# w2's raw pieces in the pool of h's loads and taps, loaded two half steps sooner

## The chip, the cores and the metric

The kernel runs on one core of one Trainium2 chip. The metric is device microseconds of one launch on that core, the median of several runs.

## What is computed

The reference adds three things for one sequence of S = 2048 rows and D = 448 columns: its input `x`, a long-convolution branch, and a two-layer MLP. F is 1792.

```python
xn = _layernorm(x)
# A: short causal convolution of k (4 taps), times v, long causal convolution by FFT, gate
k_shift = sum(k_pad[:, t:t + S, :] * shift_k[:, ks - 1 - t] for t in range(ks))
kv = k_shift * v
y = irfft(rfft(kv) * rfft(ssm_k))[:S] + kv * ssm_D
a = xn * y
# B: dense, mish, dense
h = xn @ w1 + b1
b = (h * tanh(softplus(h))) @ w2
out = x + a + b
```

## The kernel before

**Steps.** The work is cut along the MLP. The sequence is 8 chunks of 256 rows, F is 7 pairs of two 128-wide blocks, and (chunk, pair) makes 56 steps. Each step has two half steps, numbered from 0: an even half step 2i runs `g1_mm` of step i (first dense layer, 22 matmuls), the odd one 2i+1 runs `mish` of step i and then `g2_mm` of step i-2 (second dense layer, 12 matmuls; `G2_LAG = 2`). All the rest, that is layer norm, the transforms of h (the kernel `ssm_k`, transposed) and of kv, the taps and the output gate, is hung on half steps by two tables: `at(s, ...)` puts a function ahead of the MLP's work of half step s, `after(s, ...)` puts it behind. The program is recorded in that order and each engine works through its own instructions in it; nothing reorders them later.

**Split weights.** TensorE multiplies in a rounded 32-bit type. Each weight is therefore split into a rounded part and a rest: ScalarE casts the raw piece (`w1_hi` L340, and the cast of `split` L74), VectorE subtracts (`w1_lo` L345 and L347, `split` L75). w1 and w2 come in 7 raw pieces each, one per pair; in this text w1[p] and w2[p] are the pieces of pair p. The split of w1[p] stands at half step 2p-2, ahead of `g1_mm` of step p. The split of w2[p] stands behind half step 2p+3, ahead of `g2_mm` of step p in half step 2p+5. All of this happens in chunk 0; later chunks find the weights in place.

**Pools.** Raw pieces of w1, w2 and later the pieces of k share `kr`, four buffers. Pool `x` has seven buffers for h's loads, v's loads, the taps' products and `sD`. A buffer is handed on in the order in which buffers are given back, and the load that takes it over waits for the last reader of the old content.

**Queues and their semaphores.** SyncE (SP) issues nearly all loads in program order; ScalarE (ACT) issues, in between its own arithmetic, the stores of the transformed h to the scratch array `Dh` (`f1_out` L140, two DMAs each, three half steps after the transform's matmuls). A DMA signals its end on one of eight semaphores, DMAHW0 to DMAHW7. The DMAs of SP and ACT take them in turn, in program order, whatever their queue, and a DMA waits for the one that had its semaphore before, unless that wait has been made already. So each DMA may have to wait for the landing of the eighth DMA ahead of it, and behind a DMA that waits stands everything that its engine has to issue after it.

**Half steps around the change.** `f1_mm` of h's pieces (L125) in chunk 0: h[1] at half step 1, h[2] at 4, h[3] at 8, h[0] at 12. ScalarE copies and VectorE adds and subtracts the result (`f1_fold`, L131, L132, L134), and `f1_out` stores it at 4, 7, 11 and 15.

The functions touched are `w2_load` and the loop over the pairs at the end of the function:

Of the kernel before, what the change touches and what calls it, by code (L numbers as in the profile page):

```python
# [14 lines left out]
S, D, F = 2048, 448, 1792  # L15
# [23 lines left out]
def tile_kernel(ctx: ExitStack, tc, q, k, v, sk, hT, sD, w1, b1, w2, c_f1, c_g, c_gi, c_i2, out):  # L39
# [51 lines left out]
    def at(slot, fn, *args):  # L91
        plan.setdefault(int(slot), []).append((fn, args))

    def after(slot, fn, *args):
        plan2.setdefault(int(slot), []).append((fn, args))
# [7 lines left out]
    def xt():  # L103
        return sp1.tile([128, 2, D], F32, name="x", bufs=7)

    def kr():
        return sp1.tile([128, 4, CH], F32, name="kr", bufs=4)
# [225 lines left out]
    RW = {}  # L333
# [17 lines left out]
        w1_lo(p)  # L351

    def w2_load(p):
        RW["2", p] = rw = kr().rearrange("p a b -> p (a b)")[:, :2 * D].rearrange("p (a b) -> p a b", a=2)
        nc.sync.dma_start(rw, w2[:, 2 * p:2 * p + 2])

    def w2_split(p):
# [198 lines left out]
    for p in range(NP):  # L556
        if p >= 2:
            at(max(2 * p - 5, 0), w1_load, p)
        if p >= 1:
            at(2 * p - 2, w1_split, p)  # L560
        p and at(2 * p + (1 if p < 5 else 0), w2_load, p)
        after(2 * (p + G2_LAG) - 1, w2_split, p)

    for o in range(NO):
# [46 lines left out]
    w1_load(1)  # L611
    nc.sync.dma_start(b1t, b1)
    w2_load(0)
    h_load(2)
    stats, aggr, eps, power, norm, tail = ln_parts(0)
# [99 lines left out]
```

## Time and profile before

| | |
|---|---|
| runs | median 369.93 us of 3 (369.01 to 371.45) |
| the profiled execution | 370.86 us, of which 368.9 us lie between its first and last instruction |
| TensorE matmul (PE) | 360.9 us busy, 98% |
| TensorE weight load (PEld) | 292.6 us, 79% |
| VectorE (DVE) | 262.5 us, 71% |
| ScalarE (ACT) | 166.3 us, 45% |
| GpSimd (POOL) | 71.2 us, 19% |
| DMA | 79.35 MB, mean 215 GB/s |

The page gives each engine's busy time in a profiled execution of 368.9 us. PE's matmuls are pipelined and their ends are modelled, so 98% busy means that nearly no gap between matmuls is left, and not that each runs at its best. Rows of the time line give start, duration, engine, line and operation, output and inputs, and in brackets the idle time ahead of the row with what ended it. The letter q behind an engine (ACTq, SPq) marks its queue of instructions: an issue of a DMA, or a wait. "DMA kr" in a row of the chain is a transfer into a `kr` buffer.

### The profile page before, as it was taken

What the parts mean: (1) busy time and instruction counts of PE and PEld (TensorE: products, weight loads), DVE (VectorE), ACT (ScalarE), POOL (GpSimd) and SP (SyncE); (2) the same over time, 40 slices, a digit from 0 to 9 for tenths busy, and PEclk for the clock granted to TensorE, in tenths of its full rate; (3) what the DMA queues carried; (4) which work ended last, traced back from release to release, by engine and by line L of the source; (5) the groups of instructions that cost most, each with busy time, mean ns of one, the idle gap of its engine ahead of it and who ended that gap; (6) DMA issues with size and microseconds to landing.
All of it is one profiled execution on the core that took longest, in us unless ns stands there. A gap on an engine that the chain in (4) does not pass through costs nothing.

```text
span 368.9 us, 7464 instructions
## 1 busy us (share of the span) xinstructions
PE 360.9 (98%) x3128; PEld 292.6 (79%) x3128; DVE 262.5 (71%) x359; ACT 166.3 (45%) x277; POOL 71.2 (19%) x58
## 2 busy tenths in 40 slices
PE   7998999999999999999999999999999999999995
PEld 2697888978888989889868666666666889889885
DVE  5897858999998888996515657656385752897751
ACT  3757543344241443253254555556655533235450
POOL 2005000920228222611006000060000005102020
PEclk9999999999999999999999999999999999999999
DMA  7998996839496329514675598896694375949655
GB/s 241 346 285 312 358 368 184 256 105 295 105 299 214 89 66 274 170 48 101 225 244 174 194 261 238 282 301 189 209 292 125 95 248 205 419 195 276 116 66 133
DMA packets 32354, 79.35 MB, mean 215 GB/s; under 512 B 2881, under 2 KB 19138, under 8 KB 32322
## 3 DMA queue, kind: packets, MB, share of 16 engines
q1 hardware_dynamic: 20210, 44.09, 35.8%
q10 hardware_dynamic: 9776, 22.88, 22.2%
q0 software_dynamic: 2336, 11.93, 11.3%
q8 instruction: 24, 0.39, 0.4%
q14 instruction: 8, 0.07, 0.1%
HBM read 50.44 MB, written 28.44 MB: 214 GB/s over the span
## 4 chain that ended last, share of the span: by engine, by line
PE 71%; DMA 12%; DVE 9%; POOL 3%; ACT 2%; issue 2%; SPq 0%; ACTq 0%; POOLq 0%; DVEq 0%
PE pg L457 27%; PE pg L482 10%; PE pg L484 9%; PE pg L483 9%; PE pc L208 7%; DMA kr<-in_w_dram 6%; PE pc L251 4%; PE pc L125 2%; PE pc L308 2%; DMA Dh<-st 2%; DVE x L172 2%; PE pg L407 2%; POOL xn L392 2%; DMA Dkv<-st 1%; DMA av<-Dkv 1%
## 5 line engine op out<-in xcount | busy, mean ns | idle before, releaser
L465 ACT ACTIVATE a<-pg,b1t 128x256 f32<-128x256 f32 x112 | 47.1, 472 | 113.0 <-PE pg L457 88.2
L457 PE MATMUL pg<-XH,w1h 128*128 128x256 f32 x448 | 91.3, 285 | 0.9 <-ACT XH L419 0.9
L75 DVE TENSOR_TENSOR acl<-a,ach 128x512 fp32r<-128x512 f32 x56 | 38.8, 693 | 65.0 <-ACT ach L74 64.7
L457 PEld LDWEIGHTS pg<-XH,w1h 128*128 128x128 f32 x448 | 69.6, 188 | 18.9 <-issue 15.7
L482 PE MATMUL pg<-w2h,ach 128*128 128x448 f32 x224 | 83.1, 371 | 0.0
L483 PE MATMUL pg<-w2l,ach 128*128 128x448 f32 x224 | 81.3, 363 | 0.9 <-DVE w2l L75 0.9
L484 PE MATMUL pg<-w2h,acl 128*128 128x448 f32 x224 | 81.4, 363 | 0.0
L457 PE MATMUL pg<-XL,w1h 128*128 128x256 f32 x448 | 69.6, 277 | 0.2 <-DVE XL L417 0.2
L457 PEld LDWEIGHTS pg<-XL,w1h 128*128 128x128 f32 x448 | 59.4, 188 | 0.4 <-DVE XL L417 0.4
L457 PE MATMUL pg<-XH,w1l 128*128 128x256 f32 x336 | 56.8, 277 | 0.0
L482 PEld LDWEIGHTS pg<-w2h,ach 128*128 128x128 f32 x224 | 42.0, 188 | 11.7 <-issue 9.4
L457 PEld LDWEIGHTS pg<-XH,w1l 128*128 128x128 f32 x336 | 46.8, 188 | 0.0
L483 PEld LDWEIGHTS pg<-w2l,ach 128*128 128x128 f32 x224 | 42.1, 188 | 3.6 <-DVE w2l L75 1.2
L484 PEld LDWEIGHTS pg<-w2h,acl 128*128 128x128 f32 x224 | 42.1, 188 | 2.5
L388 POOL TENSOR_TENSOR rstd<-ve,mhalf 128x2 f32<-128x2 f32 (+1 forms) x9 | 8.8, 977 | 156.2 <-DVE ve L385 156.1
L74 ACT CAST ach<-a 128x512 fp32r<-128x512 f32 x56 | 34.7, 620 | 1.8
L155 POOL TENSOR_TENSOR x<-kr,skb 128x896 f32<-128x896 f32 x8 | 17.1, 2133 | 83.6 <-DVE x L154 62.4
L392 POOL TENSOR_SCALAR xn<-qt,mv,rstd 128x448 f32<-128x448 f32 x12 | 27.8, 2320 | 0.6
L172 DVE TENSOR_TENSOR x<-x 128x896 f32<-128x896 f32 x24 | 26.8, 1115 | 1.4 <-POOL x L155 0.9
L131 ACT COPY st<-pc 128x896 f32<-128x896 f32 x16 | 14.5, 906 | 14.5 <-PE pc L125 12.6
L132 DVE TENSOR_TENSOR st<-pc,st 128x896 f32<-128x896 f32 x16 | 17.4, 1088 | 3.6 <-ACT st L131 3.1
L259 ACT COPY qe<-pc 128x896 f32<-128x896 f32 x16 | 13.8, 912 | 11.0 <-PE pc L251 10.8
(70 smaller groups left out, 389.7 us busy)
## 6 DMA issues: line engine op xcount, KB each, us to landing
Dh<-st ACTq DMA_DIRECT2D x16, 448.0 KB, 6.4
Dkv<-st ACTq DMA_DIRECT2D x16, 448.0 KB, 5.1
ah<-Dh SPq DMA_DIRECT2D x8, 896.0 KB, 7.0
av<-Dkv SPq DMA_DIRECT2D x8, 896.0 KB, 6.2
E<-qe ACTq DMA_DIRECT2D x16, 448.0 KB, 5.2
e<-E POOLq DMA_DIRECT2D x8, 896.0 KB, 7.9
kr<-in_k_dram SPq DMA_DIRECT2D x10, 448.0 KB, 6.7
x<-in_v_dram SPq DMA_DIRECT2D x8, 448.0 KB, 5.2
```

Of the source, the lines that this page charges most:

```text
L74: nc.scalar.copy(h, raw)
L75: V.tensor_sub(l, raw, h)
L132: V.tensor_add(st[:, 0], e, st[:, 1])
L155: nc.gpsimd.tensor_mul(o, KR[g - u // 2], skb[:, u:u + 1].to_broadcast([128, 2, D]))
L172: V.tensor_add(KV[g], KV[g], o)
L208: nc.tensor.matmul(p[32 * t:32 * t + 32, r, :D], g[rs, t, c], a[rs, t], start=True, stop=True, tile_position=(64 * r, 32 * t))
L392: eng.tensor_scalar(xn[:, jj, :D], Q[c][:, jj], mv[:, j, 0:1], rstd[:, j:j + 1], op0=ALU.subtract, op1=ALU.mult)
L457: nc.tensor.matmul(ps[:, n], l, r, start=n_ == 0, stop=n_ == len(mm) - 1)
L465: nc.scalar.activation(a[:, n], ps[:, n], AF.Mish, bias=b1t[:, 2 * p + n:2 * p + n + 1])
L482: nc.tensor.matmul(ps, ah[:, n, cs], w2h[:, f], start=f == 0, stop=False)
L483: nc.tensor.matmul(ps, ah[:, n, cs], w2l[:, f], start=False, stop=False)
L484: nc.tensor.matmul(ps, al[:, n, cs], w2h[:, f], start=False, stop=f == NF - 1)
```

## The change

w2's raw pieces are taken from pool `x` instead of `kr`, in the same shape, and the load of piece p (1 to 6) stands at half step 2p-1. Before, it stood at 2p+1 for p up to 4 and at 2p for 5 and 6. The load of piece 0, ahead of the loop, changes its pool alone. The splits stay where they are, and no arithmetic changes.

```diff
     def w2_load(p):
-        RW["2", p] = rw = kr().rearrange("p a b -> p (a b)")[:, :2 * D].rearrange("p (a b) -> p a b", a=2)
+        RW["2", p] = rw = xt()
         nc.sync.dma_start(rw, w2[:, 2 * p:2 * p + 2])
...
-        p and at(2 * p + (1 if p < 5 else 0), w2_load, p)
+        p and at(2 * p - 1, w2_load, p)
```

What it does to SP's row of loads, from w2[0] on: before (names ending in numbers are buffers; kr_119 is w2[0], x_121 is h[2], kr_163 is w1[2], qt_165 is the input rows of chunk 1, kr_200 is w1[3], x_239 is h[3], kr_241 is w2[1], kr_243 is w1[4], kr_296 is w2[2]; in brackets the semaphores that a row waits for, the number behind the underscore being the same for all):

```order
L355 DMA kr_119<-in_w2_dram 128x896 [waits DMAHW0_49]
L111 DMA x_121<-in_hT_dram 128x896 [waits DMAHW1_49]
L337 DMA kr_163<-in_w1_dram 128x1024 [waits DMAHW2_49]
L366 DMA qt_165<-in_q_dram 128x896 [waits DMAHW3_49]
L337 DMA kr_200<-in_w1_dram 128x1024 [waits DMAHW4_49,DVE_49,Activation_49]
L111 DMA x_239<-in_hT_dram 128x896 [waits DMAHW5_49]
L355 DMA kr_241<-in_w2_dram 128x896 [waits DMAHW6_49,DVE_49,Activation_49]
L337 DMA kr_243<-in_w1_dram 128x1024 [waits DMAHW2_49,DMAHW7_49,DVE_49,Activation_49]
L355 DMA kr_296<-in_w2_dram 128x896 [waits DMAHW1_49,DMAHW0_49,DVE_49]
```

And in the changed kernel (x_119 is w2[0], x_200 is w2[1], kr_202 is w1[3], x_241 is h[3], x_243 is w2[2], kr_245 is w1[4], x_298 is w2[3], kr_300 is w1[5]):

```order
L355 DMA x_119<-in_w2_dram 128x896 [waits DMAHW0_49]
L111 DMA x_121<-in_hT_dram 128x896 [waits DMAHW1_49]
L337 DMA kr_163<-in_w1_dram 128x1024 [waits DMAHW2_49]
L366 DMA qt_165<-in_q_dram 128x896 [waits DMAHW3_49]
L355 DMA x_200<-in_w2_dram 128x896 [waits DMAHW4_49]
L337 DMA kr_202<-in_w1_dram 128x1024 [waits DMAHW5_49]
L111 DMA x_241<-in_hT_dram 128x896 [waits DMAHW6_49]
L355 DMA x_243<-in_w2_dram 128x896 [waits DMAHW7_49]
L337 DMA kr_245<-in_w1_dram 128x1024 [waits DMAHW0_49,DVE_49,Activation_49]
L355 DMA x_298<-in_w2_dram 128x896 [waits DMAHW1_49]
L337 DMA kr_300<-in_w1_dram 128x1024 [waits DMAHW2_49,DVE_49,Activation_49]
```

w2[1] now stands ahead of w1[3] and w2[2] ahead of w1[4], and neither waits for a reader of an old buffer (DVE, Activation) any more. A row that waits for semaphore n as its turn comes is also the next to signal on n: w2[2] signals on DMAHW7, where it signalled on DMAHW1 before (its row before also waits for DMAHW0, as part of taking over a buffer).

On ACT the instructions and their order stay the same, but the semaphores behind the stores of `Dh` change with the row of loads. Before, from the cast of w2[0] to the second store pair:

```order
L74 CAST w2h_85<-kr_119 128x896 [waits DMAHW0_49]
L140 DMA Dh_75<-st_209 64x2x896 [waits DVE_49]
L140 DMA Dh_75<-st_209 64x2x896
L340 CAST w1h_83<-kr_200 128x4x256 [waits DMAHW4_49]
L131 COPY st_292<-pc_257 128x896 [waits PE_49]
L465 ACTIVATE a_300<-pg1_269,b1t_80 128x256 [waits PE_49]
L465 ACTIVATE a_300<-pg1_269,b1t_80 128x256
L74 CAST ach_303<-a_300 128x512 [waits Activation_49]
L74 CAST w2h_85<-kr_241 128x896 [waits DMAHW6_49]
L340 CAST w1h_83<-kr_243 128x4x256 [waits DMAHW7_49]
L140 DMA Dh_75<-st_292 64x2x896 [waits DMAHW5_49,DVE_49]
L140 DMA Dh_75<-st_292 64x2x896 [waits DMAHW1_49]
```

And in the changed kernel:

```order
L74 CAST w2h_85<-x_119 128x896 [waits DMAHW0_49]
L140 DMA Dh_75<-st_211 64x2x896 [waits DMAHW3_49,DVE_49]
L140 DMA Dh_75<-st_211 64x2x896 [waits DMAHW7_49]
L340 CAST w1h_83<-kr_202 128x4x256 [waits DMAHW5_49]
L131 COPY st_294<-pc_259 128x896 [waits PE_49]
L465 ACTIVATE a_302<-pg1_271,b1t_80 128x256 [waits PE_49]
L465 ACTIVATE a_302<-pg1_271,b1t_80 128x256
L74 CAST ach_305<-a_302 128x512 [waits Activation_49]
L74 CAST w2h_85<-x_200 128x896 [waits DMAHW4_49]
L340 CAST w1h_83<-kr_245 128x4x256 [waits DMAHW0_49]
L140 DMA Dh_75<-st_294 64x2x896 [waits DMAHW1_49,DVE_49]
L140 DMA Dh_75<-st_294 64x2x896 [waits DMAHW3_49]
```

The wait for the landing of w2[2] stood ahead of the second store of h[2] (DMAHW1), behind the casts of w2[1] and w1[4]. It now stands ahead of the second store of h[1] (DMAHW7), and the casts of w1[3], w2[1] and w1[4] stand behind it.

## The prediction

> **What bounds the kernel now.** I read the page first, then PE's waits, then the chain of waits, then the time lines of ACT, DVE, PE and SP around its first DMA pieces.
>
> ```profile
> span 368.9 us, 7464 instructions
> PE 360.9 (98%) x3128; PEld 292.6 (79%) x3128; DVE 262.5 (71%) x359; ACT 166.3 (45%) x277; POOL 71.2 (19%) x58
> DMA  7998996839496329514675598896694375949655
> ```
>
> PE is busy for 98% of the span: matmuls are the bound, and a change that leaves every matmul alone can win only idle PE time. The DMA row says that the first six slices (55 us) are nearly full of transfers, so a load there is late when others stand ahead of it. PE's waits, in part:
>
> ```profile
> PE pg L483 <- DVE w2l L75: 0.9, 1, 0.9
> ...
> PE pc L208 <- DMA av<-Dkv: 0.3, 1, 0.3
> ```
>
> The first is the only wait of PE for a w2 piece, once, for its rest part. The second is the longest that PE has behind it, at about 190 us. The chain of waits tells where the first comes from:
>
> ```profile
> 20.06 8.35 DMA kr<-in_w_dram
> ...
> 28.44 0.58 ACTq L140
> ...
> 29.07 0.85 ACT a L465 x2
> ...
> 30.46 0.95 ACT w2h L74
> ...
> 31.43 1.39 DVE w2l L75
> ...
> 32.87 0.47 PE pg L483
> ```
>
> The load of w2[2] is issued at 20.06, as soon as its buffer is free, and lands at 28.41. The step behind it is no use of w2[2]: it is ACTq L140, the second store of h[2], which waited for that semaphore. Behind it ACT does mish, the cast and so on, and PE's L483 starts at 32.87. ACT's time line shows the same hold and an earlier pair of stores without one:
>
> ```profile
> 17.46 0.63 ACTq L140 DMA_DIRECT2D Dh<-st  x1
> ...
> 18.13 0.62 ACTq L140 DMA_DIRECT2D Dh<-st  x1
> 18.82 1.04 ACT L340 CAST w1h<-kr 128x1024 fp32r<-128x1024 f32 x1
> 19.77 0.90 ACT L131 COPY st<-pc 128x896 f32<-128x896 f32 x1
> 20.57 0.84 ACT L465 ACTIVATE a<-pg,b1t 128x256 f32<-128x256 f32 x2
> 21.44 0.62 ACT L74 CAST ach<-a 128x512 fp32r<-128x512 f32 x1
> 21.96 0.94 ACT L74 CAST w2h<-kr 128x896 fp32r<-128x896 f32 x1
> 23.61 1.05 ACT L340 CAST w1h<-kr 128x1024 fp32r<-128x1024 f32 x1 [0.70 <-DMA kr<-in_w_dram]
> 23.67 5.35 ACTq L140 DMA_DIRECT2D Dh<-st  x2
> 29.07 0.84 ACT L465 ACTIVATE a<-pg,b1t 128x256 f32<-128x256 f32 x2 [4.41 <-PE pc L125]
> ```
>
> The stores of h[1] go out at 17.46 and 18.13, and ACT casts w1[3] at 18.82 without a gap. The two stores of h[2] take 5.35 us, and ACT idles for 4.41 us. The releaser named there, a transform matmul, had long been done; the chain names the right one. What PE lost by it:
>
> ```profile
> 22.72 0.52 PE L457 MATMUL pg<-XH,w1h 128*128 128x256 f32 x3
> ...
> 25.31 0.37 PE L482 MATMUL pg<-w2h,ach 128*128 128x448 f32 x1
> 25.52 0.36 PE L483 MATMUL pg<-w2l,ach 128*128 128x448 f32 x1
> ...
> 31.45 0.47 PE L482 MATMUL pg<-w2h,ach 128*128 128x448 f32 x1
> 32.87 0.47 PE L483 MATMUL pg<-w2l,ach 128*128 128x448 f32 x1 [0.94 <-DVE w2l L75]
> ```
>
> The undisturbed second layer (step 1, at 25.31) goes from L482 to L483 in 0.21 us; for step 2 it takes 1.42 us. So that stall cost 1.2 us, a third of a percent, and it is all that better loads can win back.
>
> **The change part by part.** It adds and removes no instruction; seven loads of 448 KB stay seven.
>
> *The pool.* w2's loads wait no more for readers of `kr`. The seven pieces pass once through seven buffers of `x` and are split by half step 15, ahead of the taps, so the rotation later is as it was; no load there is asked for before its buffer is long free. I cost this at nothing, and the waits of SP that go away (SP feeds nobody but the loads) are covered by PE's matmuls. If that cover were gone, a late tap would cost what VectorE has to spare, and VectorE is 29% idle.
>
> *Earlier loads.* w2[2] lands well ahead of its split, and so do w2[3] to w2[6]. With the stall of step 2 gone PE gains 1.2 us.
>
> *The order of loads.* w2[1] goes ahead of w1[3], which lands one transfer later; w2[2] and w2[3] go ahead of w1[4] and w1[5]. When they land follows from SP's issues, and the latency of each:
>
> ```profile
> 9.58 0.33 SPq L337 DMA_DIRECT2D kr<-in_w_dram  x1
> 9.95 0.43 SPq L366 DMA_DIRECT2D qt<-in_q_dram  x1
> 11.20 0.33 SPq L337 DMA_DIRECT2D kr<-in_w_dram  x1
> 11.57 0.43 SPq L111 DMA_DIRECT2D x<-in_hT_dram  x1
> ```
>
> Landing times, from the view of DMA issues in a window around each of these four:
>
> ```profile
> kr<-in_w_dram SPq DMA_DIRECT2D x1, 512.0 KB, 6.0
> ```
> ```profile
> qt<-in_q_dram SPq DMA_DIRECT2D x1, 448.0 KB, 6.8
> ```
> ```profile
> kr<-in_w_dram SPq DMA_DIRECT2D x1, 512.0 KB, 6.8
> ```
> ```profile
> x<-in_hT_dram SPq DMA_DIRECT2D x1, 448.0 KB, 7.5
> ```
>
> They are w1[2], the input rows of chunk 1, w1[3] and h[3], and land at 15.6, 16.8, 18.0 and 19.1: queued behind each other, 448 KB take 1.1 us and 512 KB take 1.2 us. In the changed kernel the first two stay. Behind them come w2[1] at 16.8 + 1.1 = 17.9, w1[3] at 19.1, h[3] at 20.2, w2[2] at 21.3. They are issued in time for that, between 10.4 and 12, since the DMAs whose semaphores they take over have landed by then (the ones of the start, all ahead of w1[2]). w1[3] at 19.1 instead of 18.0 would delay its cast (18.82) by 0.3 us, which VectorE's own work until 19.95 hides.
>
> *The wait that moves.* This is the part that costs. In ACT's new order the second store of h[1] waits for DMAHW7, which is now w2[2]. It was issued at 18.13; now it waits until w2[2] lands, and behind it stand ACT's cast of w1[3], the copy of h[2], mish of step 2, the casts of w2[1] and w1[4]. No row shows the landing of w2[2] in the new place, so I bound it. From below: 21.3, the sum above. From above: the first store of h[1] is in the other queue at the same time, issued at 17.46, of the same size:
>
> ```profile
> Dh<-st ACTq DMA_DIRECT2D x1, 448.0 KB, 5.7
> ```
>
> If its packets take turns with those of the loads one for one, it costs w2[2] one transfer of its own size, 1.1 us: 22.4. The windows say that the transfers have room for little more at this time:
>
> ```profile
> 16.00:18.00 2.00, 1.99 (x19) 0.61 (x16) 1.89 (x3) 1.97 (x5) 0.00 (x0) 1.00 0.90 367
> 18.00:20.00 2.00, 2.00 (x19) 2.00 (x19) 1.86 (x4) 2.00 (x4) 0.00 (x0) 1.00 0.76 202
> ```
>
> At 367 GB/s, 90% busy, SP's loads fill the engines by themselves; at 18 to 20 they ran dry before, and now will not. I take 22.0, since the store's packets cannot start at once after 17.46 and share only the later part of w2[2]'s way. The Trainium skill, page "DMA: Bandwidth & Descriptors", section "Queues, rings and completion order", states that each engine goes round robin between its queues by packets. By that rule alone the landing would be 22.4 and the sum 0.4 us more than mine; by strict order of issue it would be 21.3 and 0.7 us less. No row of this trace decides between them.
>
> From the landing to ACT's next instruction it was 29.07 - 28.41 = 0.66 us. So the cast of w1[3] starts at 22.7 (instead of 18.82) and ends 1.04 later at 23.7. From there VectorE has a fixed row of six instructions, which ran back to back:
>
> ```profile
> 19.95 0.95 DVE L345 TENSOR_TENSOR w1l<-kr,w1h 128x768 fp32r<-128x768 f32 x1
> ...
> 24.12 1.08 DVE L75 TENSOR_TENSOR w2l<-kr,w2h 128x896 fp32r<-128x896 f32 x1
> ```
>
> From 19.95 to 24.12 + 1.08 = 25.20, that is 5.25 us: the rest of w1[3], the add and subtract of h[2], the rest of step 2's activations, the rest of w2[1]. Before, w2[1] was ready at 25.20, 0.3 us ahead of L483 at 25.52: no slack to speak of. ACT feeds the six in time, since each of its results is due later than it comes by the durations above (copy of h[2] at 24.6, activations at 26.0, w2[1]'s cast at 26.8, wanted at 25.2, 27.3 and 28.0). Now the row starts at 23.8 and ends at 29.0. PE first waits for w1[3] (step 3, wanted at 22.72), which costs about 1 us and lies inside the longer wait behind it: L483 of step 1 starts at 29.1 instead of 25.52, 3.6 us late. The next w2 piece, w2[2], is then no longer late: between the two rests VectorE took from 25.20 to 32.82 before, of which it idled 2.46 us for the held ACT:
>
> ```profile
> 30.59 0.69 DVE L75 TENSOR_TENSOR acl<-a,ach 128x512 fp32r<-128x512 f32 x1 [2.46 <-ACT ach L74]
> ```
>
> That leaves at most 5.2 us, so w2[2]'s rest is there by 34.2, and PE wants it at 31.66 + 3.6 = 35.2. So the stall of step 2 goes: -1.2 us. The stores of h[2] behind wait for w2[3], two transfers behind w2[2] and its share of stores, about 25.4, and ACT comes to them at 27.5: no second hold.
>
> *Sum.* +3.6 - 1.2 = +2.4 us, and nothing later gives it back: behind 33 us PE has no wait over 0.3 us that a later start could fill. The span goes from 368.9 to 371.3, the profiled execution from 370.86 to 373.2. That execution lay 0.93 us above the median of the runs shown, so for the median I forecast 369.93 + 2.4 = 372.3 us. By the steps above, each us by which w2[2] lands sooner or later moves this by 1 us.
>
> **The rivals.**
>
> *The load is early enough.* If w2[2] landed by 17.5, ACT would not be held at all, and the 1.2 us would be pure gain: 368.7. It turns at a landing of 22.0 - 2.4 = 19.6; earlier than that the kernel gets faster. For it: between 18 and 20 the transfers of before were at 202 GB/s, so there was room. Against it: four transfers stand between the input rows of chunk 1, landing at 16.8, and it, and none of the four landed in under 1.1 us behind its predecessor. The Trainium skill, same page, section "Rules for kernel authors", advises to issue a DMA early and wait on its semaphore late. By that rule the time is this rival's, but here the semaphore is also waited on early, by the store. Chance 0.13.
>
> *The loads crowd the stores.* Stores and loads share the engines worse than one for one: Dh's store took 5.7 us at a time with hardly a load beside it. If w2[2] landed as late as 24.0, the sum would be 2.4 + 2.0: 374.3 us, and a second hold, of the stores of h[2] for w2[3] and for the first store of h[1], would set in as these pass 27.5, for up to another 1.5 us: 375.8. For it: early transfers are the fullest stage. Against it: loads landed steadily. Chance 0.15.
>
> *Nothing moves.* The hold is there, but PE and VectorE have enough spare to swallow it and the gain cancels the loss: 369.4 to 370.6. This asks for a landing near 19.6 to 20.3, one transfer less than I count. Chance 0.10.
>
> **How the numbers follow.** My forecast (w2[2] lands from 20.3 to 23.5, time 370.6 to 373.8) has 0.62, the rivals 0.13, 0.15 and 0.10. The range reaches from 369.6 to 374.8: it takes in the quiet case and the first half of the crowded one, and leaves out the early one and the second hold. About 1%, 3.7 us, is what a measurement of this kernel can tell from no change. Faster by more than that is excluded by the 1.2 us that there are to win, but for a side effect that I do not see: 0.02. Slower by more than 3.7 us needs a landing after 23.3, the crowded rival and the tail of the forecast: 0.14. The rest is within 1%: 0.84.
>
> **What would show it.** Right: ACTq L140 near 18 us takes until about 22; the cast of w1[3] starts near 22.7; PE waits for w1[3] at about 22.7 and for w2[1] (L483) until about 29; the wait of L483 for w2[2] is gone; behind 36 us every matmul is 2.4 us late. Wrong: the two stores of h[1] still go out by 18.8, or PE's L457 of step 3 starts at 22.7 with no gap. A wait of PE in the stage of the taps (60 to 120 us) that was not there before would show a cost of the pool that I put at nothing.

## The result and the profile after

| | before | changed |
|---|---|---|
| median | 369.50 us of 22 (368.68 to 371.57) | 371.28 us of 22 (369.98 to 373.31) |
| the profiled execution | 370.86 us, span 368.9 | 373.31 us, span 371.5 |
| ratio of the times | | 1.0041, interval 1.0024 to 1.0057 |

The changed kernel is slower by 0.4%, 1.5 us by the ratio and 1.8 us by the medians. The clock is not the reason: four of its 22 runs have a mean granted clock of 0.994 or 0.995, and they took 370.88 to 371.75 us, among the others. The forecast was 372.3 us, 2.4 us over the median shown then. The profiled execution of the changed kernel is the slowest of its 22, which has to be kept in mind when its sizes are read.

The head of its page:

```profile
span 371.5 us, 7462 instructions
PE 362.0 (97%) x3128; PEld 292.9 (79%) x3128; DVE 262.7 (71%) x359; ACT 166.6 (45%) x277; POOL 73.0 (20%) x58
DMA  7999974848498138443676678896694374959655
```

Each engine has as many instructions counted as before, and the span is 2.6 us longer. PE is idle for 1.5 us more (371.5 - 362.0 against 368.9 - 360.9); its busy time is 1.1 us longer too, and where that goes the page doesn't say. PE's waits for weights (us in total, times, longest) say what it waited for:

```profile
PE pg L483 <- DVE w2l L75: 1.5, 1, 1.5
PE pg L457 <- ACT w1h L340: 1.1, 2, 1.0
```

There was one wait of this kind before, 0.9 us for w2[2]. Now the longest is 1.5 us, and w1 pieces are waited for too. The chain of waits shows the order:

```profile
12.00 10.16 DMA x<-in_w_dram
...
22.18 0.58 ACTq L140
22.81 1.05 ACT w1h L340
...
28.14 1.01 DVE w2l L75
29.20 0.47 PE pg L483
```

w2[2] is issued at 12.00 and lands at 22.16. The step behind that landing is once more no use of w2[2] but a store: the second store of h[1]. ACT's time line shows what stood behind it:

```profile
17.79 0.63 ACTq L140 DMA_DIRECT2D Dh<-st  x1
...
22.18 0.58 ACTq L140 DMA_DIRECT2D Dh<-st  x1
22.81 1.04 ACT L340 CAST w1h<-kr 128x1024 fp32r<-128x1024 f32 x1 [3.62 <-DMA x<-in_w_dram]
```

The first store goes out at 17.79, the second 4.4 us later (before: 17.46 and 18.13), and the cast of w1[3] waits 3.62 us for it. Further along this is VectorE's last instruction for w2[1], and PE:

```profile
28.06 1.08 DVE L75 TENSOR_TENSOR w2l<-x,w2h 128x896 fp32r<-128x896 f32 x1
```

```profile
23.91 0.62 PE L457 MATMUL pg<-XH,w1h 128*128 128x256 f32 x3 [0.95 <-ACT w1h L340]
...
24.90 0.62 PE L457 MATMUL pg<-XH,w1l 128*128 128x256 f32 x3 [0.37 <-DVE w1l L345]
...
29.20 0.47 PE L483 MATMUL pg<-w2l,ach 128*128 128x448 f32 x1 [1.54 <-DVE w2l L75]
...
35.16 0.36 PE L482 MATMUL pg<-w2h,ach 128*128 128x448 f32 x1
35.36 0.36 PE L483 MATMUL pg<-w2l,ach 128*128 128x448 f32 x1
...
37.56 0.52 PE L457 MATMUL pg<-XH,w1h 128*128 128x256 f32 x3
```

Three waits of 0.95, 0.37 and 1.54 us for w1[3] and w2[1]. The stall of step 2 is gone: L483 follows L482 in 0.20 us, at 35.36. Step 5 begins at 37.56; before it began at 35.19. That is 2.37 us of the 2.45 us between the two profiled executions, so hardly anything changes behind step 5.

### The profile page after: what moved, and what is told of

It reads as the page before. It is cut to its first block, busy times and chain, and to the rows that moved or that the text cites. A ratio compares the mean times of both kernels' runs of the same rounds, so it can differ in the third digit from the quotient of the medians.

```text
span 371.5 us, 7462 instructions
## 1 busy us (share of the span) xinstructions
PE 362.0 (97%) x3128; PEld 292.9 (79%) x3128; DVE 262.7 (71%) x359; ACT 166.6 (45%) x277; POOL 73.0 (20%) x58
## 4 chain that ended last, share of the span: by engine, by line
PE 76%; DMA 8%; DVE 7%; POOL 3%; issue 2%; ACT 1%; SPq 1%; ACTq 0%; DVEq 0%; POOLq 0%
PE pg L457 29%; PE pg L482 10%; PE pg L484 10%; PE pg L483 10%; PE pc L208 7%; PE pc L251 4%; DMA x<-in_w_dram 3%; DMA Dkv<-st 2%; DMA kr<-in_w_dram 2%; PE pc L125 2%; PE pc L308 2%; PE pg L407 2%; POOL xn L392 2%; DVE st L132 1%; POOL x L155 1%
## 5 line engine op out<-in xcount | busy, mean ns | idle before, releaser
L482 PE MATMUL pg<-w2h,ach 128*128 128x448 f32 x224 | 83.0, 371 | 0.0
L483 PE MATMUL pg<-w2l,ach 128*128 128x448 f32 x224 | 81.3, 363 | 1.5 <-DVE w2l L75 1.5
L482 PEld LDWEIGHTS pg<-w2h,ach 128*128 128x128 f32 x224 | 42.0, 188 | 11.6 <-issue 9.4
L483 PEld LDWEIGHTS pg<-w2l,ach 128*128 128x128 f32 x224 | 42.1, 188 | 4.2 <-DVE w2l L75 1.8
L392 POOL TENSOR_SCALAR xn<-qt,mv,rstd 128x448 f32<-128x448 f32 x12 | 28.6, 2389 | 0.6
L419 ACT CAST XH<-pg 128x512 fp32r<-128x512 f32 x16 | 9.4, 590 | 20.9 <-PE pg L407 19.5
```

The lines of the kernel that those rows point to most:

```text
L392: eng.tensor_scalar(xn[:, jj, :D], Q[c][:, jj], mv[:, j, 0:1], rstd[:, j:j + 1], op0=ALU.subtract, op1=ALU.mult)
L482: nc.tensor.matmul(ps, ah[:, n, cs], w2h[:, f], start=f == 0, stop=False)
L483: nc.tensor.matmul(ps, ah[:, n, cs], w2l[:, f], start=False, stop=False)
```

## The experiments

The theory: the second store of h[1] has to wait for the landing of a load, the eighth DMA ahead of it, and behind the store stands ACT's cast of w1[3]; so the time follows the landing of that load. Its rivals: the loads' new order or the pool costs PE something by itself, or the stall of step 2 is worth something other than was read.

One table first, since most verdicts use it. For each profiled execution it has its time, the start of step 5's first matmul, the time less that start, and where the store was held, the start of the second store of h[1], the end of w2[1]'s rest on VectorE and the us between the two.

| execution | us | step 5 | rest of the run | store | w2[1] ready | between |
|---|---|---|---|---|---|---|
| before | 370.86 | 35.19 | 335.67 | not held | | |
| e5, before again | 369.42 | 33.93 | 335.49 | not held | | |
| e6, before, third | 371.16 | 35.60 | 335.56 | not held | | |
| changed | 373.31 | 37.56 | 335.75 | 22.18 | 29.14 | 6.96 |
| e7, changed again | 371.19 | 35.73 | 335.46 | 20.33 | 27.29 | 6.96 |
| e12, changed, third | 371.62 | 35.97 | 335.65 | 20.58 | 27.54 | 6.96 |
| e1 | 369.25 | 33.59 | 335.66 | on GpSimd | | |
| e2 | 374.19 | 38.98 | 335.21 | 23.59 | 30.54 | 6.95 |
| e3 | 370.48 | 34.95 | 335.53 | 19.56 | 26.52 | 6.96 |
| e4 | 374.12 | 34.13 | 339.99 | not held | | |
| e8 | 370.54 | 35.16 | 335.38 | 19.77 | 26.73 | 6.96 |
| e11, e8 again | 370.88 | 35.12 | 335.76 | 19.73 | 26.69 | 6.96 |
| e9 | 370.47 | 34.36 | 336.11 | not held | | |
| e10 | 370.53 | 35.32 | 335.21 | on SP | | |

In twelve of the fourteen the rest of the run is 335.2 to 335.8 us. What a version costs is thus decided ahead of step 5, except in e4 and e9. And in all seven executions with a held store step 5 starts 15.38 to 15.40 us behind the store (37.56 - 22.18, 35.73 - 20.33 and so on), though the store itself starts anywhere between 19.56 and 23.59: where it is held, the store sets the time.

**e1: the stores of h[1] on GpSimd's queue.** In the changed kernel (here and below, "..." at the end of a line stands for the rest of it, which is unchanged):

```diff
-        nc.scalar.dma_start(...
+        (nc.gpsimd if dst is Dh and g == H_HEAD else nc.scalar).dma_start(...
```

> The changed kernel, with the two stores of h[1] issued by GpSimd, whose DMAs take no turn among the eight semaphores of SP and ACT. Theory (the store's turn holds ACT): ACT casts w1[3] as soon as it lands, at about 19.7 instead of 22.8; L483 of step 1 starts at about 25.6 instead of 29.2; PE waits for no w2 piece; the store pair of h[2] now waits for w2[2] and w2[3] and holds ACT until about 25.5, too short to matter. Time 1.2 us under the kernel before: ratio 0.997. Rival (order of the loads: w1[3] and w1[4] land late behind w2's pieces, whoever stores): nothing changes against the changed kernel: ratio 1.004, L483 at about 29.

Measured: 369.26 us, 1.0004 of before (0.9993 to 1.0016). ACT's time line:

```profile
18.20 1.05 ACT L340 CAST w1h<-kr 128x1024 fp32r<-128x1024 f32 x1
...
23.28 3.17 ACTq L140 DMA_DIRECT2D Dh<-st  x2
```

The cast of w1[3] is at 18.20 with no gap, PE waits for no weight, and the whole loss is gone, though the pool, the half steps and the order of the loads are those of the change. The loss is the hold. The store pair of h[2] takes ACT's queue 3.17 us here, and that costs PE nothing. But the gain of 0.3% expected with it did not come: without the hold the kernel is at before, and not under it.

**e2: a longer hold.** One more DMA ahead of the store, sD's load in two halves, so that the store waits for w1[4] and not for w2[2]:

```diff
-        nc.sync.dma_start(dt, sD)
+        for a in range(2):
+            nc.sync.dma_start(dt[:, 224 * a:224 * a + 224], sD[:, 224 * a:224 * a + 224])
```

> The changed kernel, with the small load of sD cut into two halves. This adds one DMA ahead of the second store of h[1], so that the store waits for w1[4] instead of w2[2]; no other load moves by more than the time of one small issue. Theory: the hold lasts until w1[4] lands, at about 24.4 instead of 22.2; cast of w1[3] at about 25.0, L483 of step 1 at about 31.4; 2.2 us slower than the changed kernel, ratio 1.010 to the kernel before. Rival (order of the loads, or the pool): as the changed kernel, ratio 1.004, L483 at 29.2.

Measured: 374.35 us, 1.0146 (1.0124 to 1.0168). Its time line (line numbers are one higher in this kernel):

```profile
23.59 0.58 ACTq L141 DMA_DIRECT2D Dh<-st  x1
24.21 1.04 ACT L341 CAST w1h<-kr 128x1024 fp32r<-128x1024 f32 x1 [5.06 <-DMA kr<-in_w_dram]
...
29.46 1.08 DVE L75 TENSOR_TENSOR w2l<-x,w2h 128x896 fp32r<-128x896 f32 x1
```

The store starts 1.41 us after that of the changed kernel's profile, w2[1] is ready 1.40 us later, step 5 starts 1.42 us later. The median came out higher than expected (1.010), probably since the store of a typical execution of the changed kernel starts earlier than 22.18 (e7, e12), so that the hold grows by more than 2.2 us. All five runs also have a lower mean clock (0.991 to 0.995); the dip behind it cost nothing in the profiled execution (last section), and whether it did in the others isn't shown.

**e3: a shorter hold.** The load of h[0] and of sD behind it stands at half step 10 instead of 7 (three half steps later, where the expectation says two), so that the store waits for h[3], one transfer ahead of w2[2]:

```diff
-        at(t - 5 if t > 7 else t - 3, h_load, g)
+        at(t - (2 if g == 0 else 5) if t > 7 else t - 3, h_load, g)
```

> The changed kernel, with the loads of h[0] and sD two half steps later, so that one DMA fewer stands ahead of the second store of h[1] and it waits for h[3], which lands one transfer ahead of w2[2]. Theory: the hold ends at about 21.0 instead of 22.2; cast of w1[3] at 21.7, L483 of step 1 at about 28.0; 1.1 us faster than the changed kernel, ratio 1.001. Rival (order of the loads, or the pool): loads up to w2[2] are unmoved, so ratio 1.004 and L483 at 29.2.

Measured: 370.41 us, 1.0028 (1.0012 to 1.0043), between the two expectations. Its time line:

```profile
19.56 0.58 ACTq L140 DMA_DIRECT2D Dh<-st  x1
20.19 1.05 ACT L340 CAST w1h<-kr 128x1024 fp32r<-128x1024 f32 x1 [1.88 <-DMA x<-in_hT_dram]
...
25.44 1.08 DVE L75 TENSOR_TENSOR w2l<-x,w2h 128x896 fp32r<-128x896 f32 x1
```

The transfer that ends the wait is h[3] (named in the bracket). The hold is shorter and again 6.96 us lie between store and w2[1]. Against e5 step 5 starts 1.02 us later, which is 0.28% of the time, and against e7 0.78 us sooner. The theory as stated had booked a gain of 1.2 us against the hold; without that gain the hold alone gives what was measured.

**e4: before, with the stores of h[2] on GpSimd.** This was to remove the one stall that the profile of before had:

```diff
-        nc.scalar.dma_start(...
+        (nc.gpsimd if dst is Dh and g == 2 else nc.scalar).dma_start(...
```

> The kernel before, with the two stores of h[2] issued by GpSimd. Theory: the hold of ACT from 24.7 to 29.1, which waits for the landing of w2[2], goes; L483 of step 2 follows L482 without the wait of 0.94 us; 1.2 us faster than the kernel before, ratio 0.997, with no change to pool or loads. Rival (w2[2] is late because its load is issued late): the load still lands at about 28.4 and the cast of w2[2] still comes at about 29 to 30, so a part of the wait for its rest stays and the ratio is 0.998 to 1.000.

Measured: 375.07 us, 1.0164 (1.0135 to 1.0193). The expectation, 0.997, missed by 2%. The stall is gone, with step 5 at 34.13, but the rest of the run is 4.5 us longer. GpSimd's time line, and ACT's:

```profile
30.09 4.72 POOL L392 TENSOR_SCALAR xn<-qt,mv,rstd 128x448 f32<-128x448 f32 x2
...
36.02 1.51 POOL L140 DMA_DIRECT2D Dh<-st  x2
```

```profile
46.53 0.91 ACT L131 COPY st<-pc 128x896 f32<-128x896 f32 x1 [4.73 <-DMA Dh<-st]
```

GpSimd issues in order too, and the layer norm of the next chunk stood ahead, which itself waited for VectorE until 28.90: the stores went out at 36.02 instead of about 24. `st` has two buffers; ACT's copy of h[0] waited 4.73 us for one of them, and PE then waited 1.13 and 1.14 us for w2 pieces; behind these waits its granted clock was at 0.57 for 4 us, so not all of the 4.5 us is waiting. The hold was not removed, it was moved to another engine and made longer.

**e5, e6, e7, e12: both kernels again.** No edit; e5 and e6 are before, e7 and e12 the changed kernel, for further profiles.

> The kernel before, unchanged, for another profiled execution. Its first profiled execution took 370.86 us against a median of 369.5. Theory (that execution had late transfers, and the wait of L483 for w2[2] is not in most executions): w2[2] lands by about 26.5 instead of 28.4, ACT is held for 2 us or less, L483 of step 2 follows L482 at once, the time is about 369.3. Rival (the wait is in every execution): landing at about 28.4, wait of about 0.9 us, time about 370.9.

> The kernel before a third time, as the run ahead of it: by the theory the time and the landing of w2[2] go together, and the time is 369.3 us plus what L483 of step 2 waits. Rival: the time varies with no relation to this wait.

> The changed kernel, unchanged, for another profiled execution. Its first one took 373.31 us against a median of 371.28, the slowest of 22. Theory: w2[2] lands at about 20 to 21 instead of 22.2, the cast of w1[3] starts 0.65 us behind that, L483 of step 1 waits and starts 7.0 us behind the landing, and the time is less than 373.3 by just as much as the landing is earlier, about 371.3. Rival (the hold is the same in every execution, the rest varies): landing at about 22, with another time.

> The changed kernel once more, unchanged, for a third profiled execution (the first two: 373.31 us with the second store of h[1] at 22.18, and 371.19 us with it at 20.33). Theory (landing of w2[2] + 6.96 us = w2[1]'s rest ready, and that sets the time): whatever the time of this execution, 370 to 373 us, the constant is 6.95 to 6.97, and the time less the distance from step 0 to step 5 is 344.1 to 345. Rival (the spread of the changed kernel comes from elsewhere): the distance differs from the time less 344.5 by over 0.6 us.

Measured: 369.42, 371.16, 371.19 and 371.62 us. e5 lies at the median of before, and its time lines (ACT, then PE) show no stall at all:

```profile
23.93 3.42 ACTq L140 DMA_DIRECT2D Dh<-st  x2
```

```profile
31.52 0.36 PE L482 MATMUL pg<-w2h,ach 128*128 128x448 f32 x1
31.72 0.36 PE L483 MATMUL pg<-w2l,ach 128*128 128x448 f32 x1
```

The store pair of h[2] took 3.42 us instead of 5.35, because w2[2] landed at 26.8 instead of 28.4, and L483 follows L482 in 0.20 us. In e6 there is a stall of 1.02 us, but another one:

```profile
18.60 2.19 ACTq L140 DMA_DIRECT2D Dh<-st  x1
20.84 1.05 ACT L340 CAST w1h<-kr 128x1024 fp32r<-128x1024 f32 x1 [1.43 <-issue]
```

Here the issue of the second store of h[1] took 2.19 us by itself (0.62 in the first profile), with no wait for a semaphore shown, and the same row of casts came late. So e6's theory, 369.3 us plus the wait of step 2, missed by 1.9 us, and its rival, a time that varies without that wait, holds. In e7 the changed kernel's store waits for w2[2], as before, but this lands 1.85 us earlier, and the time is 2.12 us shorter:

```profile
20.33 0.58 ACTq L140 DMA_DIRECT2D Dh<-st  x1
...
26.21 1.08 DVE L75 TENSOR_TENSOR w2l<-x,w2h 128x896 fp32r<-128x896 f32 x1
```

e12 has the 6.96 us too, but it meets its rival's condition, by a little: the distance from step 0 to step 5 is 35.97 - 9.54 = 26.43, and 371.62 - 344.5 = 27.12 is 0.69 more. What went wrong is the measure. PE began step 0 at 9.54, after a wait of 1.70 us for its first operand, where the other two began at 8.51 and 8.72, and from 12 to 14 us its granted clock was at 0.50. That moves the start of the distance and not its end: step 5 starts 15.39 us behind the store, as in the others. But PE was so late by itself that it waited for w2[1] for only 0.17 us (1.49 in e7):

```profile
27.60 0.47 PE L483 MATMUL pg<-w2l,ach 128*128 128x448 f32 x1 [0.17 <-DVE w2l L75]
```

So in e12 the slow clock alone would have cost nearly as much as the hold, and what the hold added can't be read from it. Taken over three executions each, step 5 starts at 36.42 (mean of 37.56, 35.73, 35.97) and before at 34.91 (35.19, 33.93, 35.60): 1.5 us apart, as the ratio is. With three executions each, one of them with that dip, this agrees with the ratio and proves no more.

**e8 and e11: the pool alone.** The changed kernel with the old half steps for the loads; e11 is the same kernel again.

```diff
-        p and at(2 * p - 1, w2_load, p)
+        p and at(2 * p + (1 if p < 5 else 0), w2_load, p)
```

> The change of pool alone: w2's pieces in pool x, their loads at the old half steps. The stores of h[1] get the same two semaphores as in the changed kernel, and the second waits for w1[4], which in this order is the eighth DMA ahead of it and takes about the place in the queue that w2[2] has in the changed kernel (sixth transfer behind w1[2], 64 KB more). Theory: ACT is held as in the changed kernel, cast of w1[3] at 21 to 23; time as the changed kernel or up to 0.3 us more, ratio 1.004 to 1.006, though no load was moved. Rival (the two half steps make the cost): ratio 1.000 or below.

> The pool alone once more, unchanged, for one more profiled execution: the first one, 370.54 us, was the fastest of its six (median 372.57). Theory (the hold is all there is, and it varies with the landing of w1[4], for which the second store of h[1] waits): a typical execution, 372 to 373 us, shows this store at 21.4 to 22.2 instead of 19.77, w2[1]'s rest ready 6.96 us behind it, and the first matmul of step 5 at 28 to 28.7 us after that of step 0 (instead of 26.41); the time less that distance is 344.1 to 345. Rival (something behind step 5 costs as well, a late load of w1 or w2 or a lower clock): the distance stays near 26.4 and the time less the distance is 345.5 or more. If this execution is again near 370.5 us it tells neither.

Measured: e8 372.57 us, 1.0092 (1.0062 to 1.0122), above the 1.004 to 1.006 expected; e11 370.88 us, which by its expectation tells neither theory. The hold is there without the two half steps. SP's load of w1[4] and ACT's rows, of e8:

```profile
11.04 0.87 SPq L337 DMA_DIRECT2D kr<-in_w_dram  x1
```

```profile
16.69 0.62 ACTq L140 DMA_DIRECT2D Dh<-st  x1
...
19.77 0.58 ACTq L140 DMA_DIRECT2D Dh<-st  x1
20.40 1.05 ACT L340 CAST w1h<-kr 128x1024 fp32r<-128x1024 f32 x1 [2.31 <-DMA kr<-in_w_dram]
```

And the same load before:

```profile
18.20 0.33 SPq L337 DMA_DIRECT2D kr<-in_w_dram  x1
```

The loads stand in the same order in SP's program in both. Before, w1[4] waited for a `kr` buffer and went out at 18.20, behind both stores of h[1] (17.46, 18.13). With the pool changed it goes out at 11.04, ahead of both, as the eighth DMA ahead of the second store. Counted over SP's and ACT's issues in order of time, the eighth ahead is the DMA that the held store waits for: w2[2] in the profiled execution of the changed kernel and in e7, w1[4] in e2 and e8, h[3] in e3. (Which DMA it is stands fixed in the program and isn't decided while it runs: in e12, where one of SP's loads goes out behind the store, it is the seventh.) So what makes the hold is that SP runs ahead of the stores, and the pool alone lets it. Why the median of e8 is 1.3 us above the changed kernel's (1.9 us by the ratios, whose intervals don't overlap) stays open; the two half steps, added to the pool, may win something back, and no run shows by what. The profiles don't help: the two, at 370.54 and 370.88 us, are both below e8's five other runs. The mean granted clock was 0.993 to 0.995 in three of e8's six runs and 1.00 in both profiles, which would go with the dips below, but no trace shows it, and one run at 1.00 took 372.55 us.

**e9: the two half steps alone.** Before, with the new half steps and the old pool:

```diff
-        p and at(2 * p + (1 if p < 5 else 0), w2_load, p)
+        p and at(2 * p - 1, w2_load, p)
```

> The two half steps alone: w2's pieces stay in pool kr, their loads stand at half step 2p-1. Both stores of h[1] then wait for DMAs that landed long ago, and the second of h[2] for h[3]: no hold of ACT at a store. But SP's loads wait for readers again: w2[2] takes w1[2]'s buffer (split done at about 18.1) and w1[4] takes w2[0]'s (about 20.3), so w1[4] lands at 26.5 to 27.5 instead of 23.6 to 24.4. Theory (the hold at the store is the whole cost of the change, and the pool brings it by letting SP run ahead): no store of ACT takes over 1.3 us ahead of 30 us; the cast of w1[4] is the one that waits, until about 27, step 1's L483 starts with no wait, and step 2's is late by 0.5 to 1 us; ratio 1.000 to 1.004. Rival (loads in the new order cost by themselves): L483 of step 1 late as in the changed kernel, ratio 1.004 to 1.006.

Measured: 370.22 us, 1.0028 (1.0011 to 1.0045). ACT's time line:

```profile
18.05 0.62 ACTq L140 DMA_DIRECT2D Dh<-st  x1
...
26.29 1.05 ACT L340 CAST w1h<-kr 128x1024 fp32r<-128x1024 f32 x1 [2.91 <-DMA kr<-in_w_dram]
```

The store goes out at 18.05: no hold, as expected of loads that still wait for `kr` buffers. w1's loads now stand behind w2's in that pool, and the cast of w1[4] waits 2.91 us for its data. PE waits for no weight in this execution, so the late L483 of step 2 that was expected did not come: from step 0 to step 5 it takes 24.93 us, as in e5 (24.95). Step 5 starts later than in e5 only because step 0 does (9.43 against 8.98). 0.3 us of PE are idle between 36 and 60 us, and where the rest of the 0.28% goes was not found. The interval leaves 1.000 out, so the half steps alone have a cost of their own, about 1 us, whose cause stays open.

**e10: the stores of h[1] and h[2] on SP.** The changed kernel with:

```diff
-        nc.scalar.dma_start(...
+        (nc.sync if dst is Dh and g in (1, 2) else nc.scalar).dma_start(...
```

> The changed kernel, with the four stores of h[1] and h[2] issued by SP instead of ACT. SP then waits for landings and for VectorE, and behind it stand loads that are wanted from 29 us on. Theory: ACT is not held before 30 us, the cast of w1[3] starts when w1[3] lands or the cast of w2[0] ends, at 18 to 19, step 1's and step 2's L483 start with no wait, g1_mm of step 5 starts 24.8 to 25.0 us behind that of step 0, as in the run with the stores of h[1] on GpSimd; time 369.2, ratio 0.998 to 1.000. If the kernel before loses 1.2 us in some of its executions and this one in none, its spread is smaller too. Rival (SP's wait makes loads late): a cast of ACT waits for w1[5] or w1[6], ratio above 1.002.

Measured: 369.01 us, 0.999 of before (0.9978 to 1.0003). Now SP waits, and it has only loads behind the stores:

```profile
20.04 1.05 ACT L340 CAST w1h<-kr 128x1024 fp32r<-128x1024 f32 x1
```

The cast has no idle time ahead of it, and PE waits for no weight. The cast is later than expected (18 to 19), and from step 0 to step 5 it takes 26.00 us instead of 24.8 to 25.0: a dip of the clock ahead of step 5, shown below, which is most of the 1.5 us by which this execution lies above its median. This is the lowest median of the versions tried, though it can't be told from before, and the spread (368.29 to 370.53) isn't clearly smaller (368.34 to 371.05).

## Why the prediction was right, and in what it was wrong

The sign, the place and the mechanism were right, and the sum was 0.6 to 0.9 us too high. By its steps:

- **The wait that moves.** Right, and in the profiled execution close in every number: landing 22.16 (22.0 forecast), cast of w1[3] 22.81 (22.7), L483 of step 1 at 29.20 (29.1). The fixed row from the held store to w2[1] is 6.95 or 6.96 us in seven executions of four kernels (7.0 forecast, counted from the landing). As a size for the median it was too large, since the landing taken was that of a late execution: in e7 and e12 it is 20.31 and 20.56. Against e5, step 5 is then 1.80 and 2.04 us late and not 3.6, the second with the dip of the clock in it. That the profiled execution, the slowest of 22, hit the forecast landing is luck.
- **Earlier loads.** The gain of 1.2 us is the term that failed. The stall of step 2 went, as forecast, but a typical execution of before doesn't have it: e5, at the median, has none, and e6 has one of 1.02 us from another cause. In the 22 runs of before 14 are below 370 us, so executions like e5 are probably the more frequent; that is argued from the times alone. e1 is the direct test: with the hold taken away nothing was won.
- **The sum.** +3.6 - 1.2 was made of two terms that both came from executions with late transfers; in typical ones they are about +1.8 and 0. The errors, 1.8 too much loss and 1.2 too much gain, partly cancel, and that the total came near is partly luck.
- **The pool.** Costed at nothing; it is the cause of the hold. e8 has the hold with the pool alone. The prediction read the new semaphore correctly from the order of instructions but put it down to the new half steps. Semaphores were said to be taken in turn in program order, whatever the queue. The rows ahead of the prediction say otherwise: both stores of h[1] stand at half step 4, so by program order only w1[4] would stand between w2[2] (DMAHW7) and them, and they would take DMAHW1 and DMAHW2. They wait for DMAHW3 and DMAHW7. So two loads of later half steps (w2[3], w1[5]) are counted ahead of the first store and three more (h[0], sD, w2[4]) ahead of the second. That is the order in which the trace of the changed kernel shows the issues: a load freed from a wait moves ahead in it. The statement that no load is asked for before its buffer is long free was wrong too: in the changed kernel SP waits 1.8 us ahead of a load of w2 for VectorE to split an earlier piece. No wait of PE comes from it.
- **The order of loads.** Nearly right: a transfer took 1.2 to 1.3 us in the profiled execution, 1.1 to 1.2 in the forecast. From issue to landing, in the changed kernel, for the input rows of chunk 1 (issued at 10.06), h[3] (11.48), w2[2] (12.00) and w1[4] (12.56):

```profile
qt<-in_q_dram SPq DMA_DIRECT2D x1, 448.0 KB, 7.0
...
x<-in_hT_dram SPq DMA_DIRECT2D x1, 448.0 KB, 9.5
x<-in_w_dram SPq DMA_DIRECT2D x1, 448.0 KB, 10.2
...
kr<-in_w_dram SPq DMA_DIRECT2D x1, 512.0 KB, 11.8
```

They land at 17.1, 21.0, 22.2 and 24.4. From the input rows to h[3] it is 3.9 us for three transfers (w2[1], w1[3], h[3]), and from h[3] to w2[2] 1.2 us, one transfer: the store issued at 17.79 took no turn ahead of w2[2]. From w2[2] to w1[4] it is 2.2 us, a transfer and about as much again. The traffic of the queues shows why. From 17.8 to 21.2 us SP's queue (q1) has 99.8% of the engines' time and ACT's (q10; ACT's 48 stores of 448 KB make 22.0 of its 22.9 MB) moves nothing. From 23 to 24 us (packets, MB, share of the 16 engines):

```profile
q10 hardware_dynamic: 59, 0.21, 51.6%
q1 hardware_dynamic: 61, 0.21, 51.3%
```

The Trainium skill, page "DMA: Bandwidth & Descriptors", section "Queues, rings and completion order", has the engines go round robin between queues by packets. The equal halves from 23 us on agree with that. But the store's packets came more than 3.4 us behind its issue, too late to slow w2[2]; why so late, no run shows. Strict order of issue was thus the better estimate: it put w2[2] 4.5 us behind the input rows, and 5.1 us were measured in this execution, 4.5 in e7 (15.77 to 20.31) and 4.6 in e12. The prediction came to 22.0 by giving the store a share of the engines ahead of w2[2]. It had next to none (ACT's queue moved 0.02 MB from 21.2 to 22.2 us): the 22.16 come from input rows that landed 0.3 us later than forecast and from four transfers behind them that took 0.6 us more.
- **The rivals.** "The load is early enough" fell: w2[2] landed at 20.31, 20.56 and 22.16 in the three profiled executions. Its turning point at 19.6 fell too, because the 1.2 us were not there to win: e3 is held until 19.56 and slower than before. "Nothing moves" had its landing almost, in e7 and e12, but not its time: with no 1.2 us to set against the loss, these took 371.19 and 371.62 us and not 370.6 or less. "The loads crowd the stores" fell for the changed kernel; e2, held until 23.59, shows what it would have cost.
- **Behind 36 us.** Right: the rest of the run is the same to 0.3 us in three executions each, and there is no new wait in the stage of the taps.

## What to carry to other kernels

Before a load is moved, read from the order of the built program which DMA each store will wait for (here the eighth ahead of it, counted over both queues that share the semaphores), and ask what computation stands behind that store on its engine. A load freed from its buffer's readers can cost time by running ahead. Read a stall from more than one execution before it is booked as a gain: one trace's 1.2 us may be a late transfer that the median run doesn't have, and a store that may have to wait does least harm on an engine with only transfers behind it: on SP (e10) it cost nothing that could be measured, on GpSimd behind a layer norm (e4) 1.6%.

## What was not expected of the hardware

**The granted clock can halve after a short wait of PE.** In e10 PE waited 1.46 us for its first operand of step 0, and then (columns of the windows: PE, PEld, DVE, ACT, POOL busy, granted clock, DMA share, GB/s):

```profile
9.32 0.62 PE L457 MATMUL pg<-XH,w1h 128*128 128x256 f32 x3 [1.46 <-ACT XH L419]
```

```profile
9.00:11.00 2.00, 1.50 (x10) 1.30 (x11) 1.96 (x4) 1.17 (x3) 0.00 (x0) 1.00 1.02 375
11.00:14.50 3.50, 3.50 (x30) 2.68 (x28) 1.67 (x3) 1.59 (x3) 0.00 (x0) 0.53 1.00 378
```

The clock falls to 0.53 in these 3.5 us. In steps of 0.25 us it is at 0.50 from 11.2 to 14.6 us, 3.4 us long. Three more executions have such a stretch of 3.4 us at 0.50: e12 from 11.4 to 14.8 us, after a wait of 1.70 us; e2 from 26.3 to 29.7, after 2.07 us, where it cost nothing, since w2[1]'s rest was ready only at 30.54 and PE came to it at 30.60; e4 from 52.5 to 55.9, after 1.13 and 1.14 us. In e11 the same wait as in e10 has no such effect:

```profile
9.37 0.62 PE L457 MATMUL pg<-XH,w1h 128*128 128x256 f32 x3 [1.45 <-ACT XH L419]
```

```profile
8.00:16.00 8.00, 6.45 (x59) 5.42 (x60) 6.00 (x10) 6.12 (x10) 0.00 (x0) 1.00 1.01 392
```

Nor had the 1.60 us that PE waited in e9 and the 1.52 us in e4, both at the same place (1.00 from 9 to 16 us). So the wait's length alone doesn't decide. The Trainium skill, page "TensorE: Matmul & The Clock Gate", Part 1, has a free-running activity window of about 3.4 us decide on half or full rate. The halved rate and the 3.4 us agree with that; the traces don't show the window itself, and here single waits of 1.46 to 2.07 us, or two of 1.1 us close together, were enough in some executions.

**An issue has no fixed price.** The same second store of h[1] takes 0.62 us to issue in before and 2.19 in e6, with no wait shown, and behind it PE waited 1.02 us for w2[1].
